# Moving two pieces of VectorE work behind the gating product: accumulator sums one step later, and the weight joins of the first two steps

## The chip, the cores and the metric

One core of one Trainium2 chip. The time is device time in microseconds (us) of one execution. The profile is of one execution of its own; its span (first to last instruction) is about 1.8 us shorter than the time of the same run.

Names: PE is TensorE (matmuls), PEld its weight loads, DVE is VectorE, ACT is ScalarE, POOL is GpSimd, SP is the engine that issues most transfers. A "q" behind a name means the engine's sequencer.

## The reference, cut to what matters

```python
# a Mamba-2 scan over chunks gives attn_out; then a gated two-layer network on it
x = attn_out.transpose(0, 2, 1, 3).reshape(3072, 256)
h = x @ w_in            # 256 -> 2048
g = h * np.cos(h)       # the gate
return g @ w_out        # 2048 -> 256
```

## The kernel before: the parts that matter

The feed-forward part runs in 96 steps, 16 in each of six chunks. Step n computes h for 256 hidden columns and 512 tokens on TensorE into one of **two** PSUM banks (`hp`), gates it, and two steps later the second layer (`second(n - 2)`) uses the result.

```python
def first(n):
    hp[n] = bank([P, TB], "hp", "h")                 # two banks
    ... 4 matmuls (8 in the profile) into hp[n] ...
    ACT.activation(k, hp[n], AF.Copy, bias=0.25, scale=INV_2PI)       # k: whole turns
    V.scalar_tensor_tensor(out=w, in0=hp[n], scalar=INV_2PI, in1=k, ...)   # w
def gate(n):  ACT.activation(cos, cos, AF.Sin, ...)                    # sine
def gated(n): V.tensor_tensor(out=gT[n], in0=hp.pop(n), in1=cos, op=ALU.mult)  # frees hp[n]
```

So the hp of step n+2 can only start when `gT` of step n has been written: the chain is hp, k (ScalarE), w (VectorE), sine (ScalarE), gT (VectorE), then the bank is free.

The weights arrive as 64-bit words and are turned into float32 piece by piece. The last part of that is a join: two VectorE operations and a GpSimd add. Even pieces are of `w_out`, odd ones of `w_in`; the first join in the loop is of `w_out`'s first piece, which `second(0)` reads.

```python
def join(which, i):
    V.tensor_scalar(out=bits, in0=bits, ...)                     # 128x512, "L207"
    V.scalar_tensor_tensor(out=bits, in0=high, in1=bits, ...)    # "L209"
    G.tensor_tensor(out=kept(which, i), in0=bits, in1=last, op=ALU.add)   # "L217"
```

From the second chunk on, the second layer forms 2x2 block products with seven multiplications in two PSUM banks. When an accumulator is finished (nine times, every eight steps), it is copied out and four sums are made on VectorE:

```python
ACT.copy(out=ps[:, 0:3], in_=o[c, u][0][:, 0:3])       # frees the first bank
V.tensor_copy(out=ps[:, 3:7], in_=o[c, u][1])          # frees the second bank
for dst, a_, b_ in (... four of them ...):
    V.tensor_tensor(out=dst, in0=a_, in1=b_..., op=ALU.add)
for s in range(2):
    nc.sync.dma_start(out=to_rows[2 * u + s, c], in_=sum_...)
```

The loop, cut:

```python
for n in range(NC * NF + LAG):
    first(n); ...; gate(n)
    if n in piece: join(*piece[n])      # n = 0..15
    gated(n)
    for do in behind: do()              # scans and masks of the next chunk
    second(n - LAG)                     # with the copies and sums when an accumulator ends
```

Of the kernel before, what the change touches and what calls it, by code (L numbers as in the profile page):

```python
# [12 lines left out]
ALU = mybir.AluOpType  # L13
# [12 lines left out]
def kernel(  # L26
# [29 lines left out]
    nc = tc.nc  # L56
    V, ACT, G, PE = nc.vector, nc.scalar, nc.gpsimd, nc.tensor
# [3 lines left out]
    P = 128  # L61
# [9 lines left out]
    W = P // 2  # L71
# [14 lines left out]
    def bank(shape, name, tag):  # L86
        return psum.tile(shape, FP32, tag=tag, bufs=2, name=name)

    def pair(name):

        return psum.tile([P, 2, 4 * P], FP32, tag="scan", bufs=2, name=name)
# [64 lines left out]
    def kept(which, i):  # L156
        return (w_in[:, :, i * WC:(i + 1) * WC] if which == "in" else
                w_out[:, i * WF:(i + 1) * WF])
# [42 lines left out]
    def join(which, i):  # L201



        parts = held.pop((which, i), ())
        for e, (high, bits, last) in enumerate(parts):
            V.tensor_scalar(out=bits, in0=bits, scalar1=3, scalar2=0x3FFFFFFF,  # L207
                            op0=ALU.logical_shift_left, op1=ALU.bitwise_and)
            V.scalar_tensor_tensor(out=bits, in0=high, scalar=0xC0000000, in1=bits,  # L209
                                   op0=ALU.bitwise_and, op1=ALU.bitwise_or)  # L210
            dst = kept(which, i)
            if len(parts) > 1:
                dst = dst[:, :, e * P:(e + 1) * P]
            else:
                bits, last = (ap.rearrange("p (k f) -> p k f", k=dst.shape[1])
                              for ap in (bits, last))
            G.tensor_tensor(out=dst.bitcast(U32), in0=bits, in1=last, op=ALU.add)  # L217

    for b in range(NB):
# [4 lines left out]
        out=a_in, in_=a.rearrange("(u b) h (c p) -> (b h c) u p", u=NU, p=P))  # L224
# [15 lines left out]
    for t in range(2):  # L240
# [30 lines left out]
                    in1=those.unsqueeze(2).to_broadcast([P, NB, W]), op=ALU.mult)  # L271
# [8 lines left out]
    for t in range(2):  # L280
        G.tensor_tensor(out=a0s[:, t, HH:H], in0=halves[:, t:t + 1].to_broadcast([P, HH, W]),
                        in1=mine[:, HH:H].unsqueeze(2).to_broadcast([P, HH, W]), op=ALU.mult)
    G.tensor_tensor(out=tos, in0=to.unsqueeze(1).to_broadcast([P, H, W]),
                    in1=mine.unsqueeze(2).to_broadcast([P, H, W]), op=ALU.mult)
# [219 lines left out]
    def turn_of(n):  # L504

        c, f = divmod(n, NF)
        return (f % 2, f // 2) if c == 0 else divmod(f, NJ)
# [20 lines left out]
    def gate(n):  # L528
        cos = turns[n]
        ACT.activation(cos, cos, AF.Sin, bias=quarter, scale=TWO_PI)  # L530
# [34 lines left out]
    to_rows = out.rearrange("(b c t i) m -> b c i t m", b=NB, c=NC, t=2)  # L565
# [22 lines left out]
    def seven(n):  # L588

        c = n // NF  # L590
        u, j = turn_of(n)
        final = n >= NC * NF - NJ
        if j == 0:


            if final:
                lo, hi = (pair("o")[:, 0].rearrange("p (q m) -> p q m", m=P) for _ in range(2))
                mid = bank([P, 4, P], "o", "o")
                o[c, u] = (mid, lo, hi, {1: mid[:, 0], 6: mid[:, 1], 7: mid[:, 2], 5: mid[:, 3],
                                         2: lo[:, 0], 3: lo[:, 1], 4: hi[:, 0]})  # L600
            else:
                lo, hi = (bank([P, 4, P], "o", "o") for _ in range(2))
                o[c, u] = (lo, hi, {1: lo[:, 0], 6: lo[:, 1], 2: lo[:, 2], 7: hi[:, 0],
                                    5: hi[:, 1], 4: hi[:, 2], 3: hi[:, 3]})
        at = o[c, u][-1]
        g = gT.pop(n)
        if n == NC * NF - 1:
            last_step(g, *o[c, u][1:3])
            return
        d = gd.pop(n)  # L610
        w = {1: w4[:, j, 0, 0], 2: w4[:, j, 1, 0], 3: w4[:, j, 1, 1], 4: wd[3][:, j],
             5: wd[0][:, j], 6: wd[2][:, j], 7: wd[1][:, j]}
        a_ = {1: g[:, 0], 2: g[:, 2], 3: d[:, 3], 4: g[:, 3], 5: d[:, 0], 6: d[:, 2], 7: d[:, 1]}
        starts = (1, 2, 4) if final else (1, 7)
        for q in (1, 2, 6, 7, 5, 4, 3):
            PE.matmul(at[q], lhsT=a_[q], rhs=w[q], start=(j == 0 and q in starts),  # L616
                      stop=(j == NJ - 1), skip_group_check=True)
        if final and j == NJ - 2:
            shared(o[c, u][0])
        if j < NJ - 1:  # L620
            return

        sum_ = two.tile([P, 7, P], FP32, tag="sum", bufs=1, name="sum")
        ps = two.tile([P, 7, P], FP32, tag="ps", bufs=1, name="ps")
        ACT.copy(out=ps[:, 0:3], in_=o[c, u][0][:, 0:3])
        V.tensor_copy(out=ps[:, 3:7], in_=o[c, u][1])
        for dst, a_, b_ in ((sum_[:, 0:2], ps[:, 1:3], ps[:, 0:1]),
                            (sum_[:, 5:7], ps[:, 3:5], sum_[:, 0:1]),
                            (sum_[:, 3:5], ps[:, 5:3:-1], sum_[:, 5:6]),
                            (sum_[:, 2:3], ps[:, 6:7], sum_[:, 6:7])):  # L630
            V.tensor_tensor(out=dst, in0=a_, in1=b_.to_broadcast([P, dst.shape[1], P]), op=ALU.add)
        for s in range(2):
            nc.sync.dma_start(out=to_rows[2 * u + s, c],
                              in_=sum_[s * W:(s + 1) * W, 1:5].rearrange(
                                  "p (t h) m -> p t (h m)", t=2))

    shares_ = {}

    def shared(mid):

        ps = two.tile([P, 7, P], FP32, tag="ps", bufs=1, name="ps")
        ACT.copy(out=ps[:, 0:4], in_=mid)
        add = dict(op=ALU.add)
        V.tensor_tensor(out=ps[:, 1], in0=ps[:, 1], in1=ps[:, 0], **add)
        V.tensor_tensor(out=ps[:, 4:6], in0=ps[:, 2:4],
                        in1=ps[:, 1:2].to_broadcast([P, 2, P]), **add)
        V.tensor_tensor(out=ps[:, 6], in0=ps[:, 4], in1=ps[:, 3], **add)

        shares_.update({0: ps[:, 0:6:5], 1: ps[:, 4:7:2]})

    def last_step(g, lo, hi):

        for t, acc in enumerate((lo, hi)):
            for e in range(2):
                PE.matmul(acc[:, 0:2], lhsT=g[:, 2 * e + t], rhs=w_out[:, NF - 2 + e],  # L655
                          start=False, stop=(e == 1), skip_group_check=True)
            ob = conv.tile([P, 2, P], FP32, tag="last", bufs=3, name="ob")
            V.tensor_tensor(out=ob, in0=acc[:, 0:2], in1=shares_[t], op=ALU.add)
            for s, eng in enumerate((nc.sync, nc.scalar)):
                eng.dma_start(out=to_rows[NB - 2 + s, NC - 1, :, t],  # L660
                              in_=ob[s * W:(s + 1) * W].rearrange("p h m -> p (h m)"))
# [28 lines left out]
    for dst, src in ((a_cut, cut), (a_all, la)):  # L690
        nc.sync.dma_start(
            out=dst.rearrange("(u b) h (c p) -> (b h c) u p", u=NU, p=P), in_=src)
# [5 lines left out]
    rest = grade("out", 0, later=True)  # L698
# [3 lines left out]
    piece = {n: ("in", (n + 3) // 2) if n % 2 else ("out", n // 2) for n in range(NF)}  # L702
# [53 lines left out]
    for n in range(NC * NF + LAG):  # L756
        c, f = divmod(n, NF)
        if n < NC * NF:
            if f == 0 and c > 0:
                load(c + 2)  # L760
            first(n)
            if n == 0:
                first_scan()
            for at in pairs(n):
                turn2(*at)
            rests = [rest] if n == 0 else []
            if n + 1 in piece:
                rests.append(grade(*piece[n + 1], later=True))
            gate(n)
            for rest in rests:  # L770
                if rest:
                    rest()
            if n in piece:
                join(*piece[n])

            behind = [lambda at=at: halved(*at) for at in halves_at(n)]
            behind = [lambda at=(c, 2 * u + 1): masked(*at) for c, u in pairs(n - 2)] + behind
            if n not in piece and behind:
                behind.pop(0)()
            gated(n)  # L780
            for do in behind:
                do()
            if n in (1, 2):
                carry(0, n - 1, sums[n - 1])
        for i, js in differ_at.get(n, ()):
            differ_w(i, js)
        if n >= LAG:
            second(n - LAG)
        for c, u in pairs(n - 1):
            intra2(c, u)  # L790
            masked(c, 2 * u)
        for c, us in ends(n):
            finish2(c, us)
            if 1 in us:
                raw.pop(c)
        for c, u in pairs(n + 1):
            for b in (2 * u, 2 * u + 1):
                reaches(c, b)
                load_along(c + 1, (b,))
# [30 lines left out]
```

## Time and profile before

| | before |
|---|---|
| time, median of 3 runs | 382.38 us (382.20 to 382.62) |
| span of the profiled run | 380.8 us |
| TensorE, VectorE busy | 98%, 73% |

The lines themselves are in the prediction below. How to read them: TensorE's row of matmuls gives start, modelled duration, line, output and inputs, and in brackets idle time and what ended it. As matmuls overlap in the listing, short waits do not show as idle time; the distance between the starts of neighbouring groups shows them.

### The profile page before, as it was taken

How to read it: one execution, taken by the hardware profiler on the slowest of the kernel's cores; microseconds unless marked ns; L12 is line 12 of the kernel's file. 1: busy time of each engine (PE TensorE's matmuls, PEld its weight loads, DVE VectorE, ACT ScalarE, POOL GpSimd, SP SyncE). 2: the span in 40 equal slices, each digit the busy share in tenths (PEclk: the TensorE clock that was granted, in tenths of full speed). 3: DMA queues.
4: the chain of work that ended last, by engine and by line, in shares of the span. 5: the costliest groups of instructions: out<-in, count | busy, mean ns of one | idle time of the engine just before them, and what ended most of it. 6: DMA issues, size and time to landing. Idle time of an engine off the chain costs nothing.

```text
span 380.8 us, 7676 instructions
## 1 busy us (share of the span) xinstructions
PE 373.8 (98%) x2980; PEld 330.6 (87%) x2980; DVE 279.7 (73%) x431; ACT 172.4 (45%) x303; POOL 212.7 (56%) x330
## 2 busy tenths in 40 slices
PE   8989999999999999999999999999999999999995
PEld 2568888889989899998899998899998999999995
DVE  8898999799699748877648976756976862644643
ACT  3877666544334433443434453424444433433442
POOL 5776555479863436773544683543685343354451
PEclk9999999999999999999999999999999999999999
DMA  7988989969222961420941330100100100000101
GB/s 82 262 242 269 256 204 131 180 93 169 87 84 80 109 61 58 137 72 2 109 45 57 83 118 9 41 2 2 28 3 3 28 2 2 13 17 0 29 0 28
DMA packets 106370, 30.41 MB, mean 80 GB/s; under 512 B 75520, under 2 KB 102240, under 8 KB 106336
## 3 DMA queue, kind: packets, MB, share of 16 engines
q1 hardware_dynamic: 106176, 29.81, 39.2%
q8 instruction: 23, 0.38, 0.5%
q10 hardware_dynamic: 160, 0.13, 0.1%
q14 instruction: 11, 0.09, 0.1%
HBM read 26.59 MB, written 3.34 MB: 79 GB/s over the span
## 4 chain that ended last, share of the span: by engine, by line
PE 96%; DVE 1%; ACT 1%; POOL 1%; issue 0%
PE hp L519 44%; PE o L616 33%; PE o L578 7%; PE g L423 3%; PE y L457 3%; PE y L450 1%; PE tp L406 1%; PE a_ps L299 1%; PE warm L101 1%; PE o L655 1%; PE s_ps L478 0%; PE l_ps L318 0%; PE g L374 0%; PE tp L360 0%; DVE mag L207 0%; DVE mag L209 0%
## 5 line engine op out<-in xcount | busy, mean ns | idle before, releaser
L519 PE MATMUL hp<-yT,w_in 128*128 128x256 f32 x768 | 184.0, 382 | 1.8 <-DVE gT L535 1.4
L519 PEld LDWEIGHTS hp<-yT,w_in 128*128 128x128 f32 x768 | 139.4, 190 | 22.9 <-issue 5.0
L560 POOL TENSOR_TENSOR gd<-gT 128x256 f32<-128x256 f32 x79 | 59.5, 753 | 103.5 <-DVE gT L535 73.9
L530 ACT ACTIVATE w<-w,quarter 128x512 f32<-128x512 f32 x96 | 69.3, 722 | 84.4 <-DVE w L525 84.3
L525 DVE SCALAR_TENSOR_TENSOR w<-hp,k 128x512 f32<-128x512 f32 x96 | 65.6, 683 | 53.1 <-ACT k L523 53.0
L523 ACT ACTIVATE k<-hp 128x512 int32<-128x512 f32 x96 | 57.1, 594 | 99.0 <-PE hp L519 98.9
L535 DVE TENSOR_TENSOR gT<-hp,w 128x512 f32<-128x512 f32 x96 | 65.1, 678 | 30.6 <-ACT w L530 28.0
L616 PE MATMUL o<-words,gd 128*128 128x128 f32 x474 | 66.9, 277 | 0.0
L616 PEld LDWEIGHTS o<-words,gd 128*128 128x128 f32 x474 | 59.8, 192 | 0.5
L345 DVE TENSOR_TENSOR_SCAN lam<-arow,unit 128x512 f32<-128x512 f32 x40 | 55.7, 1394 | 0.0
L616 PEld LDWEIGHTS o<-w_out,gT 128*128 128x128 f32 x316 | 46.9, 191 | 3.6
L563 POOL TENSOR_TENSOR gd<-gT,gd 128x128 f32<-128x128 f32 x79 | 46.0, 582 | 6.2
L616 PE MATMUL o<-w_out,gT 128*128 128x128 f32 x316 | 48.0, 274 | 0.0
L562 POOL TENSOR_TENSOR gd<-gT,gd 128x128 f32<-128x128 f32 x79 | 42.7, 540 | 6.2
L616 PE MATMUL o<-words,gT 128*128 128x128 f32 x158 | 30.6, 275 | 0.0
L616 PE MATMUL o<-w_out,gd 128*128 128x128 f32 x158 | 30.6, 275 | 0.0
L578 PE MATMUL o<-w_out,gT 128*128 128x256 f32 x128 | 30.2, 379 | 0.0
L578 PEld LDWEIGHTS o<-w_out,gT 128*128 128x128 f32 x128 | 24.2, 190 | 3.3
L436 DVE TENSOR_TENSOR m<-g,lam 128x512 f32<-128x512 f32 x40 | 25.5, 679 | 0.0
L616 PEld LDWEIGHTS o<-words,gT 128*128 128x128 f32 x158 | 24.0, 192 | 0.0
L616 PEld LDWEIGHTS o<-w_out,gd 128*128 128x128 f32 x158 | 24.0, 192 | 0.0
L328 POOL TENSOR_TENSOR sc<-bc,lam 128x128 f32<-128x128 f32 x20 | 8.3, 417 | 14.4 <-DVE lam L345 7.3
(91 smaller groups left out, 290.9 us busy)
## 6 DMA issues: line engine op xcount, KB each, us to landing
arow<-a_cut SPq DMA_DIRECT2D x20, 512.0 KB, 3.9
words<-in_moe_w_in_dram SPq DMA_DIRECT2D x8, 512.0 KB, 5.8
words<-in_moe_w_out_dram SPq DMA_DIRECT2D x8, 512.0 KB, 9.3
out_dram<-sum SPq DMA_DIRECT2D x18, 128.0 KB, 2.6
xr<-in_x_dram SPq DMA_DIRECT2D x4, 512.0 KB
along<-a_all SPq DMA_DIRECT2D x20, 64.0 KB
xr<-in_x_dram SPq DMA_DIRECT2D x8, 128.0 KB
bc<-in_B_dram SPq DMA_DIRECT2D x4, 256.0 KB, 5.2
```

The lines of the kernel that those rows point to most:

```text
L345: V.tensor_tensor_scan(out=lam[c, b][:, hs].rearrange("p h i -> p (h i)"), data0=rows_.rearrange("p h i -> p (h i)"), data1=unit.rearrange ...
L436: V.tensor_tensor(out=of[0], in0=g[q][:, :, s * 2 * P:(s + 1) * 2 * P], in1=of[1], op=ALU.mult)
L519: PE.matmul(to_[:, e], lhsT=w_in[:, k, fs], rhs=y[:, k, u], start=(k == 0), stop=(k == KT - 1), skip_group_check=True)
L523: ACT.activation(k, hp[n], AF.Copy, bias=0.25, scale=INV_2PI)
L525: V.scalar_tensor_tensor(out=w, in0=hp[n], scalar=INV_2PI, in1=k, op0=ALU.mult, op1=ALU.subtract)
L530: ACT.activation(cos, cos, AF.Sin, bias=quarter, scale=TWO_PI)
L535: V.tensor_tensor(out=gT[n], in0=hp.pop(n), in1=cos, op=ALU.mult)
L560: G.tensor_tensor(out=d[:, 0:2], in0=g[:, 1:2].to_broadcast([P, 2, P]), in1=g[:, 3::-3], op=ALU.subtract)
L562: G.tensor_tensor(out=d[:, 2], in0=g[:, 0], in1=d[:, 0], op=ALU.subtract)
L563: G.tensor_tensor(out=d[:, 3], in0=g[:, 2], in1=d[:, 2], op=ALU.subtract)
L578: PE.matmul(o[c, u][:, t], lhsT=g[:, 2 * e + t], rhs=w_out[:, 2 * j + e], start=(j == e == t == 0), stop=(j == NJ - 1 and e == 1), skip_gr ...
L616: PE.matmul(at[q], lhsT=a_[q], rhs=w[q], start=(j == 0 and q in starts), stop=(j == NJ - 1), skip_group_check=True)
```

## The change

Its intent: let gT run as soon as its sine is there. In steps 0 and 1 a join stood ahead of gT, and at nine accumulators four sums stood ahead of the next step's w.

```diff
         ACT.copy(out=ps[:, 0:3], in_=o[c, u][0][:, 0:3])
         V.tensor_copy(out=ps[:, 3:7], in_=o[c, u][1])
-        (four sums, two output transfers)
+        def rest():
+            (four sums, two output transfers)
+        unsummed.append(rest)
 ...
-            if n in piece:
+            if n in piece and n > 1:
                 join(*piece[n])
 ...
             gated(n)
-            for do in behind:
+            if n < 2:
+                join(*piece[n])
+            for do in (*behind, *unsummed):
                 do()
+            unsummed.clear()
```

More of the change, by code (lines that the diff above doesn't have):

```diff
@@ L626, in seven @@
         V.tensor_copy(out=ps[:, 3:7], in_=o[c, u][1])
-        for dst, a_, b_ in ((sum_[:, 0:2], ps[:, 1:3], ps[:, 0:1]),
-                            (sum_[:, 5:7], ps[:, 3:5], sum_[:, 0:1]),
-                            (sum_[:, 3:5], ps[:, 5:3:-1], sum_[:, 5:6]),
-                            (sum_[:, 2:3], ps[:, 6:7], sum_[:, 6:7])):
-            V.tensor_tensor(out=dst, in0=a_, in1=b_.to_broadcast([P, dst.shape[1], P]), op=ALU.add)
-        for s in range(2):
-            nc.sync.dma_start(out=to_rows[2 * u + s, c],
-                              in_=sum_[s * W:(s + 1) * W, 1:5].rearrange(
-                                  "p (t h) m -> p t (h m)", t=2))
+        def rest():
+            for dst, a_, b_ in ((sum_[:, 0:2], ps[:, 1:3], ps[:, 0:1]),
+                                (sum_[:, 5:7], ps[:, 3:5], sum_[:, 0:1]),
+                                (sum_[:, 3:5], ps[:, 5:3:-1], sum_[:, 5:6]),
+                                (sum_[:, 2:3], ps[:, 6:7], sum_[:, 6:7])):
+                V.tensor_tensor(out=dst, in0=a_, in1=b_.to_broadcast([P, dst.shape[1], P]),
+                                op=ALU.add)
+            for s in range(2):
+                nc.sync.dma_start(out=to_rows[2 * u + s, c],
+                                  in_=sum_[s * W:(s + 1) * W, 1:5].rearrange(
+                                      "p (t h) m -> p t (h m)", t=2))
+        unsummed.append(rest)
+    unsummed = []
     shares_ = {}
```

## The prediction

> **What bounds the kernel now.** I read the page first, then the waits of TensorE, then the timelines of TensorE and VectorE at the two places that the change touches: the first steps of the feed-forward part (20 to 32 us) and the end of one accumulation (147 to 160 us).
>
> ```profile
> span 380.8 us, 7676 instructions
> ...
> PE 373.8 (98%) x2980; PEld 330.6 (87%) x2980; DVE 279.7 (73%) x431; ACT 172.4 (45%) x303; POOL 212.7 (56%) x330
> ...
> PE 96%; DVE 1%; ACT 1%; POOL 1%; issue 0%
> ```
>
> TensorE is busy for 98% of the span and makes 96% of the chain that ended last. VectorE at 73% has room on average. So a change of order on VectorE can only win what TensorE still waits, and I have to find those waits. The list of TensorE's waits has one over 0.4 us after the start-up: a matmul of hp waits 1.4 us for gT. It is here (timeline of TensorE's matmuls):
>
> ```profile
> 21.40 1.99 PE L519 MATMUL hp<-yT,w_in 128*128 128x256 f32 x8
> 24.83 1.97 PE L519 MATMUL hp<-yT,w_in 128*128 128x256 f32 x8 [1.43 <-DVE gT L535]
> 26.63 1.89 PE L578 MATMUL o<-w_out,gT 128*128 128x256 f32 x8
> ```
>
> The first row is step 1's hp, the second step 2's, the third the first second-layer product, step 0's. There are two hp banks, so step 2 needs step 0's bank back, and gT of step 0 is what gives it back. VectorE at that time:
>
> ```profile
> 21.35 0.68 DVE L525 SCALAR_TENSOR_TENSOR w<-hp,k 128x512 f32<-128x512 f32 x1
> 21.95 1.12 DVE L207 TENSOR_SCALAR mag<-mag 128x512 uint32<-128x512 uint32 x1
> 23.10 0.98 DVE L209 SCALAR_TENSOR_TENSOR mag<-words,mag 128x512 uint32<-128x512 uint32 x1
> 24.00 0.68 DVE L535 TENSOR_TENSOR gT<-hp,w 128x512 f32<-128x512 f32 x1
> 24.61 0.68 DVE L525 SCALAR_TENSOR_TENSOR w<-hp,k 128x512 f32<-128x512 f32 x1
> ```
>
> The two middle rows (L207, L209) are a join; they stand ahead of gT, whose sine ScalarE had finished at 22.06 + 0.72 = 22.78.
>
> From 24.83 to 371 us TensorE is marked busy without a hole, but the modelled matmul time (379 ns for 256 columns) is longer than the spacing in a stream (1.73 us for eight, 216 ns each). A wait under some 0.16 us is therefore hidden in "busy". I took the start-to-start distances of equal groups from 60 us on and looked for those longer than the shortest. Near an accumulator's end they are these (TensorE, then VectorE):
>
> ```profile
> 153.92 0.39 PE L616 MATMUL o<-w_out,gd 128*128 128x128 f32 x2
> 154.21 1.97 PE L519 MATMUL hp<-yT,w_in 128*128 128x256 f32 x8
> 156.01 0.61 PE L616 MATMUL o<-w_out,gT 128*128 128x128 f32 x4
> ...
> 157.35 0.39 PE L616 MATMUL o<-w_out,gd 128*128 128x128 f32 x2
> 157.57 1.68 PE L519 MATMUL hp<-yT,w_in 128*128 128x256 f32 x7
> ```
>
> ```profile
> 149.73 0.63 DVE L631 TENSOR_TENSOR sum<-ps 128x256 f32<-128x256 f32 x1
> 150.39 1.35 DVE L631 TENSOR_TENSOR sum<-ps,sum 128x256 f32<-128x256 f32 x3
> 151.67 0.68 DVE L525 SCALAR_TENSOR_TENSOR w<-hp,k 128x512 f32<-128x512 f32 x1
> 152.27 1.21 DVE L345 TENSOR_TENSOR_SCAN lam<-arow,unit 128x512 f32<-128x512 f32 x1
> 153.40 0.66 DVE L535 TENSOR_TENSOR gT<-hp,w 128x512 f32<-128x512 f32 x1
> 153.98 0.68 DVE L525 SCALAR_TENSOR_TENSOR w<-hp,k 128x512 f32<-128x512 f32 x1
> 154.58 1.43 DVE L345 TENSOR_TENSOR_SCAN lam<-arow,unit 128x512 f32<-128x512 f32 x1
> 155.94 0.66 DVE L535 TENSOR_TENSOR gT<-hp,w 128x512 f32<-128x512 f32 x1
> ```
>
> From 153.92 to the next hp is 0.29 us where the same pair elsewhere takes 0.22 (157.35 to 157.57), and the eight after it take 1.80 instead of 1.73. Together 0.14 to 0.15 us lost, because gT ended at 153.40 + 0.66 = 154.06, just ahead of the hp that needs its bank. It came late because the sums (149.73 to 151.67) stood ahead of w, though ScalarE's k for that w was there at 149.41 + 0.60 = 150.01. The same loss shows at 214 and 274 us: three times, always at an accumulator that ends in the middle of a chunk, where a scan also stands in the step.
>
> **What the Trainium skill says.** "Perfetto Trace Analysis", section "Summary: the profiler window per engine type", says that TensorE's end is an estimate. The trace agrees: two groups above overlap by 0.16 us in the listing; so I count starts. The same page, section "Tensor Engine Instruction", calls VectorE, ScalarE and GpSimd strict FIFO. The trace agrees: gT, ready at 22.78, starts only at 24.00 behind the join. "SBUF — State Buffer", section "Who interferes with whom", says that a VectorE operation with two SBUF inputs, or in a two-port mode, excludes a GpSimd operation that reads SBUF. The trace agrees in part: a 128x128 gd operation takes 456 ns by the median, but 1.25 to 1.40 us beside a scan, and L207 above took 1.12 us (shortest 0.41) beside a GpSimd add from 21.51 to 22.78. Beside the sums, which have two SBUF inputs, it took only 0.51 us.
>
> **The change, first part: the join behind gT in steps 0 and 1.** No instruction is added or removed. In step 0, w ends at 21.35 + 0.68 = 22.03. An idle VectorE has 0.86 us between w's end and gT's start (that is the wait in front of gT wherever nothing stands between), so gT runs 22.89 to 23.57. The hp of step 2 followed gT's end by 24.83 - 24.68 = 0.15; it will start at 23.72, which is 1.11 us earlier. That is not the gain. The next thing TensorE does is the second-layer product of step 0, which reads w_out's first piece, and that piece comes from the join which has just been moved back. L207 23.5 to 23.95 (0.41 to 0.45, GpSimd free from 23.54), L209 to 24.64 (0.69 when GpSimd is free), GpSimd's add 0.15 later and 1.27 long: 24.79 to 26.06. TensorE picks that up 0.05 to 0.08 later, at 26.13. Before, it was at 26.63. A group that starts after a wait takes 1.80 to the next one instead of 1.73, so step 3's hp starts at 27.93 instead of 28.36: **0.43 us gained**, and some 0.7 of the 1.11 given back to the new wait.
>
> Step 1: w cannot run before the first join is done, 24.6, where it also ran before; gT of step 1 ends near 26.8, its bank is needed at 27.9. The second join (w_in for step 4) ends near 27.9, with the add near 29.3, and step 4 reads it at 31.4. Step 2's w falls back from 27.52 to some 28.1, and its gT to 30.0 to 30.7; its bank is needed at 31.4. From step 3 on VectorE has waits of 0.6 to 0.9 us for ScalarE and has caught up. So no second loss.
>
> **Second part: the sums one step later.** Four operations of 0.63 + 1.35 us less overlap, 1.94 us, nine times, move behind the next gT. The copies that free the accumulator's banks stay. At the accumulator of 149 us: w starts when k is there, 150.07, scan to 151.96, gT 151.9 to 152.55 instead of 154.06; the bank is needed at about 154.0, so the 0.15 us go. Now the sums run 152.5 to 154.45, next w 154.45 instead of 153.98, the scan to 156.4, gT 156.4 to 157.05 instead of 156.60. Its bank is needed by a weight load at some 157.3, with 0.12 for the signal: 0.15 us to spare. At the six other accumulators TensorE waits for no hp, and there is nothing to win; at 178 us w and gT are then followed by sums and reach scans, and the next w comes near 183.3 as before. So **3 x 0.15 = 0.45 us**.
>
> Left as it is: at seven of the nine accumulators a weight group takes 0.12 to 0.18 us longer (149.59 in the trace), because the new accumulator's second bank is freed by the VectorE copy, which stays at its place. That is 1.1 us in all which the change leaves.
>
> Sum: 0.43 + 0.45 = 0.88 us. TensorE is without a hole from there to the end, so it arrives: 382.38 - 0.88 = **381.5 us**.
>
> **The rivals.**
> - The whole wait of 1.1 us goes, because w_out's piece comes sooner than I think: with the 0.45, 380.8 us. Against it: the join and its add take 0.41 + 0.69 + 1.27 us and cannot start before gT.
> - The first gain is given back fully: L207 or L209 is held up by GpSimd again (1.12 and 0.98 us as before). Then the add ends 0.3 to 1.0 us later; the start would be equal or up to 0.5 us slower: 381.9 to 382.4 us. For it: both were slowed in this trace. Against it: GpSimd has nothing to do from 23.54 until that join is finished, as its next operations follow in order.
> - The loss at the sums moves one step on: 0.15 us of room is little, and gd of that step is exposed to the scan that follows, with 0.2 us of room by my count. That leaves 0 to 0.45 of the second part: 381.5 to 382.0 us.
> - Sums meet gd on GpSimd in the new place. In the trace they slow it by 0.05 us per operation; gd would be ready by 154.6 and is read at 156.2.
> - The output transfers start 3 us later. They take 2.6 us and nothing waits for them but the end; the last moved ones are over 20 us ahead of it.
>
> **Range and chances.** The runs before spread by 0.4 us, half of what I expect to gain. With the first rival at the low end and the second and third at the high end, 381.0 to 382.2 us should hold it 8 times in 10. 2% are 7.6 us, more than all TensorE waits together: within 2% 0.98, faster and slower 0.01 each.
>
> **What would show it.** gT of step 0 near 22.9 and no wait for gT at step 2; in its place a wait of second-layer step 0 for GpSimd's w_out of about 0.7 us; step 3's hp at 27.9. At 154, 214 and 274 us (all 0.4 to 0.9 earlier) the distance 0.22 and then 1.73, and no new longer one in the two steps after. The group at 149.6 still stretched. I am wrong if the first second-layer product starts later than 26.6, if the stretch comes back one step later, or if the gain at 30 us is gone at 60 us.

## The result, and the profile after

Ratios here are the mean time of one kernel's fast runs over that of the other's of the same rounds, so not quite the ratio of the medians quoted.

| comparison | before, median | changed, median | ratio (95%) |
|---|---|---|---|
| first, 4 runs each | 382.50 (382.20 to 382.71) | 380.65 (380.45 to 381.19) | 0.9954 (0.9937 to 0.9972) |
| second, 11 and 6 runs | 382.65 (381.90 to 383.23) | 381.41 (380.70 to 381.95) | 0.9969 (0.9956 to 0.9982) |

In the first comparison the medians are 1.85 us apart, 0.88 us had been predicted, and 380.65 us lies below the predicted range of 381.0 to 382.2. (That the difference stays within 2% was predicted too, and holds for every run told here.) In the second, with the same source again, the ratio of means is worth 1.2 us.

The page of the changed kernel, first execution:

```profile
span 379.4 us, 7680 instructions
...
PE 373.6 (98%) x2980; PEld 330.4 (87%) x2980; DVE 279.8 (74%) x431; ACT 173.6 (46%) x303; POOL 213.5 (56%) x330
```

The counted work is the same (431 VectorE operations), but there are four instructions more in all. They are semaphore waits on VectorE, 581 instructions in place of 577 when its waits and drains are counted too; they will matter.

The start, TensorE's matmuls of the changed kernel:

```profile
21.34 1.99 PE L519 MATMUL hp<-yT,w_in 128*128 128x256 f32 x8
23.49 1.97 PE L519 MATMUL hp<-yT,w_in 128*128 128x256 f32 x8 [0.16 <-DVE gT L535]
25.88 2.00 PE L578 MATMUL o<-w_out,gT 128*128 128x256 f32 x8 [0.42 <-POOL w_out L217]
27.71 1.89 PE L519 MATMUL hp<-yT,w_in 128*128 128x256 f32 x8
```

The same four groups started at 21.40, 24.83, 26.63 and 28.36. Step 2's hp is 1.34 us earlier, its wait for gT has gone from 1.43 to 0.16 us, and a new wait, for w_out's piece from GpSimd, stands in front of the second-layer product. What is left at step 3's hp is 0.65 us, of which 0.07 was there at step 0's hp already. VectorE and GpSimd at that place:

```profile
21.19 0.68 DVE L525 SCALAR_TENSOR_TENSOR w<-hp,k 128x512 f32<-128x512 f32 x1
22.65 0.69 DVE L535 TENSOR_TENSOR gT<-hp,w 128x512 f32<-128x512 f32 x1 [0.79 <-ACT w L530]
23.26 0.42 DVE L207 TENSOR_SCALAR mag<-mag 128x512 uint32<-128x512 uint32 x1
23.71 0.69 DVE L209 SCALAR_TENSOR_TENSOR mag<-words,mag 128x512 uint32<-128x512 uint32 x1
```

```profile
24.55 1.27 POOL L217 TENSOR_TENSOR w_out<-mag,last 128x512 uint32<-128x512 uint32 x1 [1.35 <-DVE mag L209]
```

gT now waits for nothing but its sine; the join follows, in 0.42 and 0.69 us where it had taken 1.12 and 0.98; the add ends at 25.82, and TensorE starts 0.06 later.

The accumulator's end, TensorE and then VectorE of the changed kernel:

```profile
153.27 0.39 PE L616 MATMUL o<-w_out,gd 128*128 128x128 f32 x2
153.49 1.89 PE L519 MATMUL hp<-yT,w_in 128*128 128x256 f32 x8
155.22 0.61 PE L616 MATMUL o<-w_out,gT 128*128 128x128 f32 x4
```

```profile
149.39 0.69 DVE L525 SCALAR_TENSOR_TENSOR w<-hp,k 128x512 f32<-128x512 f32 x1 [0.24 <-ACT k L523]
...
151.13 0.67 DVE L535 TENSOR_TENSOR gT<-hp,w 128x512 f32<-128x512 f32 x1
151.71 0.42 DVE L633 TENSOR_TENSOR sum<-ps 128x256 f32<-128x256 f32 x1
152.16 1.89 DVE L633 TENSOR_TENSOR sum<-ps,sum 128x256 f32<-128x256 f32 x3
153.97 0.68 DVE L525 SCALAR_TENSOR_TENSOR w<-hp,k 128x512 f32<-128x512 f32 x1
154.57 1.21 DVE L345 TENSOR_TENSOR_SCAN lam<-arow,unit 128x512 f32<-128x512 f32 x1
155.71 0.66 DVE L535 TENSOR_TENSOR gT<-hp,w 128x512 f32<-128x512 f32 x1
```

0.22 us to the hp and 1.73 us through it: the lost 0.15 us are back. gT of this step ended at 151.80 (154.06 before). The next gT ends at 156.37; its bank is next used at 156.78, with the weight load at about 156.67.

**Where the time went, by stretches of the trace.** I cut every trace at three points that are starts of TensorE groups: step 0's first hp matmul, step 3's first hp matmul, the last eight matmuls. The columns are the stretch lengths in us; the closing one runs to the end of the span.

| trace | start to step 0's hp | to step 3's hp | to the last matmuls | closing | VectorE instructions |
|---|---|---|---|---|---|
| before | 18.05 | 10.31 | 346.45 | 5.95 | 577 |
| before, again (e4) | 17.72 | 10.22 | 346.46 | 5.94 | 577 |
| changed | 17.98 | 9.72 | 346.04 | 5.66 | 581 |
| changed, again (e3) | 17.64 | 9.92 | 346.03 | 5.66 | 581 |
| joins only (e1) | 17.89 | 9.82 | 346.47 | 5.95 | 577 |
| sums only (e2) | 17.92 | 10.31 | 346.04 | 5.66 | 581 |

The second stretch falls with the joins, the third with the sums, as predicted. The closing stretch falls by 0.28 us too, with the sums, and that no step of the prediction had. The first stretch is the same code in all of them and scatters: over the 14 traces from 17.58 to 18.90 us.

The closing 0.28 us can be seen in VectorE's part of the end. Each row: line, sequencer, instruction, count, then shortest, median and longest duration in ns, first and last start. First before, then the changed kernel:

```profile
L825 DVEq DRAIN  x2: 120/292/464, 376.9 to 380.4; - x2
L825 DVEq EVENT_SEMAPHORE  x2: 21/21/21, 379.9 to 380.7; - x2
```

```profile
L834 DVEq DRAIN  x2: 19/242/464, 375.8 to 379.0; - x2
L834 DVEq EVENT_SEMAPHORE  x2: 21/21/21, 378.9 to 379.4; - x2
```

At the end all engines meet. VectorE is released at 379.9 and does its DRAIN only at 380.4, in 120 ns; in the changed kernel it is released at 378.9 and does it at 379.0, in 19 ns. The records behind these rows, counted from the landing of the last output: the release is at 0.42 us in both, the DRAIN at 0.90 before and 0.53 after. What follows waits for it, and the end comes 0.28 us sooner.

### The profile page after: what moved, and what is told of

Read it like the earlier page. It is cut to its first block, busy times and chain, and to the rows that moved or that the text cites. A ratio compares the mean times of both kernels' runs of the same rounds, so it can differ in the third digit from the quotient of the medians.

```text
span 379.4 us, 7680 instructions
## 1 busy us (share of the span) xinstructions
PE 373.6 (98%) x2980; PEld 330.4 (87%) x2980; DVE 279.8 (74%) x431; ACT 173.6 (46%) x303; POOL 213.5 (56%) x330
## 4 chain that ended last, share of the span: by engine, by line
PE 96%; DVE 2%; POOL 1%; issue 0%; POOLq 0%
PE hp L519 43%; PE o L616 33%; PE o L578 7%; PE g L423 3%; PE y L457 3%; PE y L450 1%; PE tp L406 1%; PE a_ps L299 1%; PE warm L101 1%; DVE mag L209 1%; PE g L374 1%; POOL w_in L217 1%; PE o L661 1%; PE s_ps L478 0%; PE l_ps L318 0%; DVE mag L207 0%
## 5 line engine op out<-in xcount | busy, mean ns | idle before, releaser
L633 DVE TENSOR_TENSOR sum<-ps,sum 128x256 f32<-128x256 f32 (+1 forms) x27 | 16.7, 645 | 0.6
```

## The experiments

The state of belief after the first two traces. Theory 1: up to the last matmul the change is worth about 1.06 us (joins and sums as predicted, a bit more), and the rest of the 1.85 is outside TensorE's stream. Theory 2: the whole difference is the work of one of the two parts.

### e1 and e2: each part alone; e3 and e4: the changed kernel and the one before once more

e1 has only the lines of the diff with `join`, e2 only those with `unsummed`; e3 and e4 are the two kernels unchanged. All four in five rounds.

> Only the joins of steps 0 and 1 behind gT. Theory 1 (what the two traces show up to the last matmul: 0.65 us at the start of which 0.07 was there before the change, 0.4 us at the sums; the rest of the measured 1.75 us is scatter of the runs outside TensorE's stream, at the start or at the end): 0.5 to 0.7 us below before, step 3's hp at 27.7 to 27.9 us, the three stretched hp distances near 154, 214 and 274 us still there. Theory 2 (the measured 1.75 us is all real and the untraced 0.7 us belongs to the joins): 1.3 us below before.

> Only the sums one step later. Theory 1: 0.4 to 0.45 us below before; step 2's hp still waits for gT 1.4 us, none of the three stretched distances left. Theory 2b (the untraced 0.7 us belongs to the sums, for instance since the output transfers land in another place): 1.1 us below before.

> The changed kernel once more, five rounds, and a second trace. Theory 1: about 1.1 us below before of the same rounds, and in the trace the last layer's final matmuls again 1.0 us earlier than in the trace of before; the 1.75 us of the first comparison was partly scatter. Theory 2: 1.7 us again, and the second trace shows where it is.

> The kernel before against itself, to see what the comparison makes of no difference and how far two traces of one kernel lie apart at 18 us, at the last matmul and at the end. Theory 1: a ratio within 0.2% of 1, but single runs up to 0.5 us apart, with the differences in the first 20 us and in the end behind the last matmul. Theory 2: runs agree within 0.2 us, so that 0.7 us cannot be scatter.

| run | median (6 runs) | ratio to before (95%) |
|---|---|---|
| e1 joins only | 382.47 | 0.9995 (0.9982 to 1.0008) |
| e2 sums only | 381.77 | 0.9981 (0.9969 to 0.9992) |
| e3 changed | 381.41 | 0.9969 (0.9956 to 0.9982) |
| e4 before | 382.68 | 1.0006 (0.9993 to 1.0020) |

The kernel before against itself gives runs from 381.9 to 383.35 us, so single runs scatter by more than the effect, and e1's ratio (0.2 us) cannot tell 0.0 from 0.6. The traces can, as the table of stretches shows: 10.3 to 9.8 with the joins alone, 346.45 to 346.04 with the sums alone. Theory 1 holds with one correction: the closing stretch is not scatter. It is 5.94 or 5.95 us in the three traces without moved sums and 5.66 us in the three with them. With it e2 is worth 0.42 + 0.28 = 0.70 us, and it measured 0.7. Theory 2 for the joins (1.3 us) has fallen. Theory 2b was right in part: 0.28 us of what had not been traced does belong to the sums. Its 1.1 us lies inside e2's interval (0.3 to 1.2 us), and only the trace speaks against it.

### e5: the closing stretch and the number of VectorE instructions

Two things go with the short closing stretch: the moved sums, and 581 instead of 577 VectorE instructions. e5 is the kernel before with nothing moved:

```diff
             for do in behind:
                 do()
+            if 40 <= n < 44:
+                V.memset(spare[:, n - 40:n - 39], 1.0)
```

> The kernel before with four one-column memsets on VectorE, steps 40 to 43, and nothing else. In the first six traces the time from the last transfer's landing to the end is 1.23 to 1.24 us in the three kernels with 577 VectorE instructions and 0.95 us in the three with 581, where VectorE's closing DRAIN is 0.28 to 0.3 us sooner behind the landing and an 8 KB instruction transfer falls before the end instead of behind it. Theory A (it is the count of VectorE instructions, whatever they do): that time falls to 0.95 us here too, the matmul stream from step 3's hp to the last matmul stays at 346.4 us, and the run is 0.28 us shorter. Theory B (it belongs to the moved sums themselves, for instance to their output transfers): it stays at 1.23 us.

Stretches: 17.82, 10.32, 346.48 and closing 5.67 us; 581 instructions; landing to end 0.95 us. The start and the stream are those of before, and the closing is that of the changed kernel:

```profile
L828 DVEq DRAIN  x2: 19/242/464, 376.7 to 379.9; - x2
```

Four memsets that nobody needs shorten the program's end by 0.28 us. The run's ratio was 0.9970 (0.9950 to 0.9989), 381.69 us median: 0.4 to 1.9 us, so more than the 0.28 us that its trace shows, and the rest is not traced. Theory B has fallen, and theory A holds in this: added VectorE instructions are enough, whatever they do. It was too simple as a count: e7 and e11 below have 572 and the short closing, too. That the place of the end in VectorE's instruction stream decides is how I read it; it is not shown directly. Over all 14 traces the long one came with 577 (before, e1, e4, e12) and the short one with 572, 581, 582 and 617.

What fetches the instructions is seen a little. The queue tables (kind, packets, MB, share) of before, then of e5:

```profile
q14 instruction: 11, 0.09, 0.1%
```

```profile
q14 instruction: 12, 0.10, 0.1%
```

In e5 one more 8 KB instruction transfer lies inside the span, 5 us ahead of the end. The Trainium skill, "Runtime: NRT & Kernel Launch", section "Instruction fetch mechanics", says that engines stream their instructions in blocks by transfers of their own, and that the cost of crossing a block is mostly hidden. Here it would be a case in which it is not hidden, 0.37 us of delay in front of the DRAIN. That the queue goes with VectorE can be seen: in all 14 traces its last transfer starts when VectorE has begun 572 to 578 of its instructions, 26 us ahead of the end in e10, which has 36 more of them. That the delay is this fetch is not shown. In the trace of before, the transfer starts only 0.3 us behind the end, so the DRAIN cannot have waited for its data; and in e11, also short, it falls about 1.7 us behind the end. What the DRAIN waited for stays open.

### e6 and e8: the start, if w_out's piece comes sooner

The new wait in the changed kernel is for the first w_out piece. e6 lets `second(0)` begin with half of it:

```diff
 def join(which, i):            # for ("out", 0) only
     V.tensor_scalar(...)
-    V.scalar_tensor_tensor(bits ...); G.tensor_tensor(dst ...)
+    for r in range(2):
+        h = slice(r * WC, (r + 1) * WC)
+        V.scalar_tensor_tensor(bits[:, h] ...)
+        G.tensor_tensor(dst[:, r] ...)
```

> The changed kernel with the first w_out piece's combine and add cut in two halves, so that the first half is there some 0.9 us sooner. If w_out's piece is the only thing that holds the start back: the first second-layer product follows step 2's hp directly at 25.3 us (25.9 in the changed kernel, all counted with step 0's hp at 18.0), step 3's hp at 27.0 instead of 27.7 us, and 0.69 us are kept to the end. If, as I read the changed kernel's trace, gT of step 2 (ending 30.8 us, its bank needed at 30.95) is the next limit right behind it: step 3's hp at 27.0 but step 4's hp at 31.0 as in the changed kernel, with a new wait of 0.5 to 0.7 us for gT, and next to nothing gained at the end.

TensorE in e6, whose step 0 is 0.92 us late against the changed kernel's (18.90 against 17.98):

```profile
24.51 1.97 PE L529 MATMUL hp<-yT,w_in 128*128 128x256 f32 x8 [0.26 <-DVE gT L545]
26.32 1.89 PE L588 MATMUL o<-w_out,gT 128*128 128x256 f32 x8
28.04 1.89 PE L529 MATMUL hp<-yT,w_in 128*128 128x256 f32 x8
29.77 1.89 PE L588 MATMUL o<-w_out,gT 128*128 128x256 f32 x8
32.04 1.97 PE L529 MATMUL hp<-yT,w_in 128*128 128x256 f32 x8 [0.38 <-DVE gT L545]
```

The wait for the piece is gone, step 3's hp is 9.14 us behind step 0's (9.72 in the changed kernel), and step 4's is 13.14 (13.18): all of it lost again in a new wait for gT. That was the expectation's second reading. It shows both that the piece was what held the start of the changed kernel, and that nothing more was to be had there alone. (The run measured 0.9974, 0.9953 to 0.9995.)

e8 tries to lift that too: the join of step 1 goes between w and gT of step 2, and that of step 2 behind gT of step 2.

```diff
-            if n in piece and n > 1:
-                join(*piece[n])
+            if n in piece and n > 1:
+                join(*piece[n if n > 2 else 1])
...
-            if n < 2:
+            if n in (0, 2):
                 join(*piece[n])
```

> The changed kernel with the first w_out piece in halves, the join of step 1 moved on to between w and gT of step 2, and the join of step 2 behind gT of step 2. By the reading that gT of step 2 is the next limit: step 3's hp at 27.0, step 4's at 30.5, no wait for gT or a piece over 0.1 us, and 0.65 us less at the end than the changed kernel. The risk is w_out's second piece, needed at 32.0 and expected at 31.4: if it is late, 0.2 to 0.4 us are left of it.

Step 3's and step 4's hp came 9.04 and 12.49 us behind step 0's, as hoped, and then it failed. VectorE and GpSimd of e8, then TensorE:

```profile
28.66 0.68 DVE L545 TENSOR_TENSOR gT<-hp,w 128x512 f32<-128x512 f32 x1
29.27 1.11 DVE L208 TENSOR_SCALAR mag<-mag 128x512 uint32<-128x512 uint32 x1
30.41 0.69 DVE L220 SCALAR_TENSOR_TENSOR mag<-words,mag 128x512 uint32<-128x512 uint32 x1
```

```profile
28.83 1.27 POOL L227 TENSOR_TENSOR w_in<-mag,last 128x512 uint32<-128x512 uint32 x1 [0.62 <-DVE mag L220]
31.18 1.27 POOL L227 TENSOR_TENSOR w_out<-mag,last 128x512 uint32<-128x512 uint32 x1 [1.09 <-DVE mag L220]
```

```profile
32.51 1.99 PE L588 MATMUL o<-w_out,gT 128*128 128x256 f32 x8 [0.37 <-POOL w_out L227]
```

The first join operation (L208 here) started beside GpSimd's add of the other piece and took 1.11 us instead of 0.41, and the second w_out piece came at 32.45 where I had expected 31.4: 0.70 us of the delay are this operation's. VectorE's w of step 3 was late behind it, step 5's hp came 16.74 us behind step 0's (16.63 in the changed kernel), and the rest was 0.6 us longer than the changed kernel's. Ratio 0.9981 (0.9959 to 1.0003). By e6 and e8, shifting joins about in this stretch only moves the loss.

### e9: only the join of step 0 moved

The changed kernel with `if n < 2` made `if n == 0` (and the other condition to match).

> The changed kernel, but only the join of step 0 stands behind gT; the join of step 1 is back ahead of it. Theory: all of the start's gain is step 0's. From step 0's hp to step 3's hp 9.6 to 9.9 us as with both joins moved (10.2 to 10.3 before). Rival: step 1's bank is late again as its gT waits for the join: 10.2 to 10.3 us, the gain gone.

9.88 us from step 0's to step 3's hp: the gain is there without step 1's move. TensorE shows a small price, 1.99 us from step 0's second-layer product to step 3's hp (25.47 to 27.46) where the changed kernel has 1.83, and 3.53 us from there to step 4's hp where it has 3.45. So in this one trace step 1's move is worth 0.16 + 0.08, about 0.2 us.

### e10: the sums made twice, to measure the room in their new place

`2 * (...)` around the four sums of the changed kernel; same result.

> The changed kernel with the four sums done twice (same result), some 2 us more of VectorE behind gT at each of nine accumulators. If the new place has only some 0.2 to 0.3 us of room at the three accumulators that end in the middle of a chunk, as the changed kernel's trace reads (gT 156.37, its bank needed at 156.67), each of the three loses about 1.8 us two steps on, 5 to 6 us in all, and the other six lose little (under 0.5 us each). If VectorE has room there in plenty: nothing is lost.

387.16 us, and 352.43 us in the third stretch against 346.04: 6.4 us lost. VectorE, then TensorE:

```profile
153.96 0.41 DVE L633 TENSOR_TENSOR sum<-ps 128x256 f32<-128x256 f32 x1
154.40 1.08 DVE L633 TENSOR_TENSOR sum<-ps,sum 128x256 f32<-128x256 f32 x3
155.41 0.68 DVE L525 SCALAR_TENSOR_TENSOR w<-hp,k 128x512 f32<-128x512 f32 x1
```

```profile
156.55 0.39 PE L616 MATMUL o<-w_out,gd 128*128 128x128 f32 x2
157.95 1.32 PE L519 MATMUL hp<-yT,w_in 128*128 128x256 f32 x5 [1.01 <-DVE gT L535]
```

The distance to the hp is 1.40 instead of 0.22 us. The second set of sums put off w by 1.44 us (153.97 to 155.41) and the loss here is 1.26 with the 0.08 in the hp behind it, so the place had about 0.2 us of room. The sum of 5 to 6 us was near, but its split was not: the three lost 1.25 us each and not 1.8. Of the other six, two in the last chunk, where no scan stands between, lost 1.1 us each, at 341 and 368 us, where I had given them under 0.5; one lost 0.4 us, at 127 us, and three lost nothing.

### e7 and e11: the copies on ScalarE (the version that beats both)

The prediction had left 1.1 us at seven weight groups that are stretched after an accumulator's end. e7 is the changed kernel with one word changed:

```diff
         ACT.copy(out=ps[:, 0:3], in_=o[c, u][0][:, 0:3])
-        V.tensor_copy(out=ps[:, 3:7], in_=o[c, u][1])
+        ACT.copy(out=ps[:, 3:7], in_=o[c, u][1])
```

> The changed kernel with the second copy of each finished accumulator on ScalarE behind the first instead of on VectorE behind gT. If the seven stretched weight groups (0.12 to 0.18 us, 1.1 us in all) wait for this copy to free the second bank: all seven go, the stream from step 3's hp to the last matmul is 1.1 us shorter than the changed kernel's (346.04 to about 344.9 us), and k of the next step is not late. If they wait for something else, for instance gd: they stay. VectorE then has at least nine instructions fewer, so by theory A of the run with four memsets the closing stretch may go back from 0.95 to 1.23 us.

> The version that should beat both kernels, once more with five rounds: the changed kernel with both accumulator copies on ScalarE. Stream from step 0's hp to the last matmul 354.6 us (356.7 before), the closing part 5.66 us (5.95 before), so 2.4 us below before: a ratio of 0.9937.

The stretched group of before, then the same group in e7, and e7's ScalarE:

```profile
149.59 0.98 PE L616 MATMUL o<-words,gd 128*128 128x128 f32 x6
```

```profile
148.55 0.83 PE L616 MATMUL o<-words,gd 128*128 128x128 f32 x6
```

```profile
147.06 0.46 ACT L625 COPY ps<-o 128x384 f32<-128x384 f32 x1
147.42 0.59 ACT L626 COPY ps<-o 128x512 f32<-128x512 f32 x1
148.37 0.60 ACT L523 ACTIVATE k<-hp 128x512 int32<-128x512 f32 x1 [0.36 <-PE hp L519]
```

The second bank is free at 148.01 instead of behind gT and a copy (149.80 before), and k still waits for its hp, so ScalarE had the room. In before, the first late matmul of the group starts at 149.86, 0.06 us behind the copy's end. All seven are gone: the third stretch is 344.98 us in both traces, 1.06 below the changed kernel. The closing stayed at 5.66 us. Ratios to before: 0.9931 (0.9913 to 0.9949) at 380.08 us, and 0.9952 (0.9937 to 0.9967) at 380.82 us; expected was 0.9937. They ran in rounds with the kernel before, not with the changed one; that they beat the changed one too rests on the traces. From step 0's hp to the last matmuls it is 354.58 and 354.81 us; 355.76 and 355.95 us in the changed kernel's two traces, 356.76 and 356.68 us in those of before.

### e12: the kernel before with only that copy moved

> The kernel before with the second accumulator copy on ScalarE, and neither part of the change. If the copy and the sums together are what makes the next w late, taking the copy's 0.6 us off VectorE ends gT near 153.4 instead of 154.06, ahead of the 154.0 when its bank is needed: the three stretched hp distances go as well as the seven stretched weight groups, and the stream from step 3's hp to the last matmul is 346.45 - 0.42 - 1.06 = 345.0 us, the same as with the sums moved. If the sums' place is needed for it: 345.4 us. The start stays as before (10.2 to 10.3 us from step 0's to step 3's hp).

344.98 us in the third stretch, exactly that of e7, with the sums still in their old place; start 10.32, closing 5.96 us (577 instructions). VectorE:

```profile
149.62 0.41 DVE L631 TENSOR_TENSOR sum<-ps 128x256 f32<-128x256 f32 x1
150.13 1.82 DVE L631 TENSOR_TENSOR sum<-ps,sum 128x256 f32<-128x256 f32 x3
151.88 0.68 DVE L525 SCALAR_TENSOR_TENSOR w<-hp,k 128x512 f32<-128x512 f32 x1
152.48 1.21 DVE L345 TENSOR_TENSOR_SCAN lam<-arow,unit 128x512 f32<-128x512 f32 x1
153.61 0.66 DVE L535 TENSOR_TENSOR gT<-hp,w 128x512 f32<-128x512 f32 x1
```

In this trace the bank is used next at 154.52, just 0.25 us behind gT's end at 154.27, and the distance from the group ahead is 0.22: no loss. So it was copy and sums together that made gT late; either one taken away is enough. Ratio 0.9964 (0.9950 to 0.9979).

## Why the prediction was right or wrong

**First part, the joins: mechanism right, size somewhat low.** Predicted were gT near 22.9, a wait for w_out's piece in place of the one for gT, and 0.43 us left at step 3's hp. All three were seen; the new wait is 0.6 us by the starts (2.39 us from hp to product instead of 1.80), where 0.7 had been said. The gain by the mean of the traces is 0.55 us: five with the joins in their old place give 10.30 us from step 0's to step 3's hp, six with both behind gT 9.75. But the six scatter from 9.59 to 9.92, in part because the join ahead of step 0's w, which the change leaves alone, ran faster in some traces than in others. Where its two operations took 0.82 and 0.69 us, the stretch is 10.31 or 10.32 without and 9.82 or 9.83 (e1, e11) with the change; where they took 0.43 and 0.98, 10.22 (e4) and 9.72 (changed). Like with like the joins are worth 0.49 to 0.50 us. The term that was off is the gap from w to gT, 0.79 us and not 0.86: just the 0.07 that 0.43 lacks. The rest of the 0.55 is scatter. The rival "fully given back" did not come; e6 shows that the rival "the whole 1.1 us" could not, as gT of step 2 was the next limit.

**Second part, the sums: right.** 0.45 predicted, 0.42 measured (346.45 to 346.04), in the three places named, with nothing lost one step later. The room was given as 0.15 us; e10 puts it near 0.2. That it came so close is partly luck, for two errors cancelled. The sums took 2.34 us in the new place and not 1.94, beside GpSimd's gd; the scan behind the next w then had GpSimd idle beside it and took 1.21 us and not the 1.43 counted. So gT ended at 156.37, which with the 0.65 us that everything had moved ahead is 157.02; 157.05 had been worked out.

**The step that failed** is the one behind the sum: "TensorE is without a hole from there to the end, so it arrives". It took all that is not TensorE's stream for constant. The stream's gain did arrive (0.97 us by the means), but the closing stretch was 0.28 us shorter as well. Splitting the sums off had added four wait instructions on VectorE, and e5 shows that four added VectorE instructions alone do this; why they do is not shown. Together 0.55 + 0.42 + 0.28 = 1.25 us (1.2 with the joins like with like), and the second comparison gives 1.2. The prediction had not thought of the number of instructions as something that costs.

**The range** was too narrow for a second reason. It was made of three runs that lay 0.4 us apart, and its low end of 381.0 us left out the first rival's own 380.8. With more runs one kernel spreads over 1.3 us, and the traces put the scatter into the stretch before step 0's hp (17.58 to 18.90). The first comparison's 380.65 us lies 0.35 us below the range, the second's 381.41 inside it. The first ratio's interval (1.1 to 2.4 us gained) contains the 1.25; the 0.5 us by which its means differ from that are not traced to anything, and stay open.

**The left-over 1.1 us** was right in size and cause: 1.06 us, by the copy that frees the second bank (e7, e12).

## What to carry to other kernels

Ask of a moved operation what will be waited for next: here the data of the moved join, then the next gT, then VectorE slowed beside GpSimd, and less than half of the first gain (0.6 of 1.3 us) could be kept. When two operations together make a third one late, look which of them an idle engine can take: one copy on ScalarE did in the stream what moving four sums did, and 1.06 us more. Below half a per cent compare traces by stretches between fixed instructions: for one order of work they repeat to 0.03 us in the middle, while whole times scatter by 1.3 us and can change when instructions that do nothing useful are added.

## What the Trainium skill lacked or had wrong

- "Runtime: NRT & Kernel Launch", section "Instruction fetch mechanics": nothing there says that the end of a program can depend on how many instructions an engine was given. Four traces with 577 VectorE instructions took 1.23 to 1.24 us from the last landing to the end, ten with 572, 581, 582 or 617 took 0.95; four idle memsets changed one into the other. It speaks of refills in 16 KiB blocks; the instruction transfers of q8 in the trace are of that size, those of q14, the queue that goes with VectorE, of 8 KB.
- "SBUF — State Buffer", section "Who interferes with whom": it calls the shared port an exclusive lock, whose loser blocks fully. For the join beside GpSimd's add the numbers are of that kind (1.11 or 1.12 us against 0.41), but beside the sums, which have two SBUF inputs, GpSimd's 128x128 operations took 0.51 to 0.52 us against 0.46, and three sums 1.89 us beside them against 1.08 with GpSimd free. Both were slowed, but the third sum, 0.28 us alone, began 0.13 us into a GpSimd operation of 0.52 us and ended 0.15 us behind it, so in the trace's windows, which are rough on GpSimd, it did not stand still until the other was done.
